# Linear attention with two gated MLPs on one core: prepared inputs through a DRAM scratch, their low halves on VectorE, output decays by a scan, two queues of work pinned

## The chip, the cores and the metric

The kernel runs on one core of a Trainium2 chip. The metric is device time in microseconds (us) of one execution, the median of several runs. The engines are named as in the profile: PE (TensorE, matrix products), PEld (its weight loads), DVE (VectorE), ACT (ScalarE), POOL (GpSimd), SP (SyncE, which here issues every DMA).

## What is computed

Inputs are six tensors of shape (4 batches, 8 heads, 768 steps, 40) and the weights of two MLPs. The first part is a recurrence over the 768 steps, for each of the 32 (batch, head) pairs, on a 40x40 state; its output, as 3072 tokens of 320 features, goes through two MLPs (320 to 2048 to 320), the second one with the gate h - tanh(h).

```python
for t in range(S):                                   # _attn_ref
    y[:, :, t] = np.einsum('bhd,bhde->bhe', rt, state)
    Sa = np.einsum('bhde,bhe->bhd', state, at)
    state_decay = state * wt[:, :, None, :] - np.einsum('bhd,bhe->bhde', Sa, bt)
    state = state_decay + np.einsum('bhd,bhe->bhde', vt, kt)
...
h = x @ w_in; g = h * (1.0 / (1.0 + np.exp(-h))); x = g @ w_out     # _moe_ref
h = x @ w_in; g = h - np.tanh(h);                 return g @ w_out  # _moe2_ref
```

## The kernel before

**Tiling.** The 768 steps are cut into 12 chunks of 64. Inside a chunk the recurrence becomes matrix products and one triangular inverse for each of the 32 pairs. A chunk is handled in two halves (hf) of 16 pairs; PE works on quarters (b = 0 to 3) of 8 pairs. Numbers that need more than half precision are kept as two f16 values, a high half (the rounded value) and a low half (what the rounding left), so that one f16 product over 120 rows holds three terms.

**The two stages.** Stage 1 runs the 12 chunks of the recurrence and, behind each chunk, the first MLP on its 256 tokens. Stage 2 (from `load_x2` on) is the second MLP for all 12 groups. The weights of both MLPs arrive as 64-bit floats and are taken apart and rebuilt by `conv_f32`, 32 conversions for each MLP, in stage 1; those of the second MLP are stored to a DRAM tensor `w2d` and read back at the start of stage 2.

**One chunk**, in the order of its data:
- `load_raw` (L195): SP loads a, (k, b), (r, v) and w of a half as 120 x 6 x 64 (120 = 3 groups of 40 features).
- `prep` (L210) for a half: DVE scans w into the running decay (L224) and its inverse (L230), multiplies a and (k, b) with them (L229, L233); POOL scales r and v (L193); ACT writes the high halves in f16 into the tile `HL`; POOL subtracts the low halves (`psub`, L190, and L239). Twelve SP transfers of 40 partitions each (L250) lay three planes (high, high or low, low) under each other in the tile `LR`, of which there are five buffers, two for a chunk. Four more transfers (L258) store the decay to the DRAM tensor `pd`. There is one buffer of `HL`.
- `p1` (L270): PE products of `LR`, taken out by DVE as `mK` (L278) and by ACT as `bP`. There is one PSUM buffer between PE and these.
- `sol_in`, 31 times `sol_step`, `sol_out` (L303 to L328): the triangular inverse on DVE. A transposition of `bP` into `Al` (L305) begins it; each step is a product (L314) and a sum (L316), 62 instructions in one chain; a transposition into `W1` (L326) ends it. `Al` and `Tl` have one buffer, so the inverse of the next chunk waits for this one's end.
- `mrg1`, `mrg2` (L334, L348), then the chain over chunks: `ch_x` (L364), `ch_u`, `ch_s`, `ch_y` (L423 to L432), `ch_m`. The buffer of `LR` is free when `ch_y` of its chunk and half has read it.
- `pf_load` (L483) reads the decay back from `pd` in three transfers in another layout, and `x_t2` (L506) multiplies the transposed output with it. Then `mm_h` (L569) and `mm_o` (L591) are the first MLP.

**Order.** Every step has a due time from the table `SC`, in units of an eighth of a chunk; steps are written in that order, and a scheduler then places each instruction on its engine's queue. Each queue runs in its order. `tc.issue_after(x)` holds what is written inside it behind instruction x on x's engine, without a wait for x's end. In the kernel before only the conversions of the first MLP are held that way (`conv_w1`, behind the first chunk's work). Those of the second (`conv_w2`, L553) have due times alone, and run between 197 and 605 us.

## Time and profile before

| | us |
|---|---|
| median of 3 runs (1231.36 to 1233.86) | 1231.57 |
| the profiled execution, its own time | 1226.61 |
| its span, from the first to the last instruction | 1224.9 |
| of the span: to the first inverse (L305 of chunk 0) | 38.6 |
| the inverses of chunks 0 to 11 (first L305 to last L326) | 747.3 |
| from there to the first product of stage 2 | 89.4 |
| stage 2 | 349.6 |

A row of the profile that groups instructions reads: line, engine, operation, output<-inputs, shapes, count | busy us, mean ns of one | idle time of the engine just before them and what ended it. Engines overlap, so that busy times do not add up to the span. A wait says which instruction an engine stood before, and whose end let it go.

### The profile page before, as it was taken

The page shows a single profiled execution, that of the slowest core. Times are in us where ns is not written, and L with a number is a line of the kernel's source. Part 1 is how long each engine was busy: PE and PEld are TensorE (multiplying, and loading weights), DVE is VectorE, ACT ScalarE, POOL GpSimd, SP SyncE. Part 2 cuts the span into 40 slices and gives each one's busy share as a digit, 9 for nine tenths or more (in the row PEclk, how much of TensorE's full clock was granted, in tenths as well). Part 3 has the DMA queues.
Part 4 walks back from the last instruction along what each step waited for, and adds up shares of the span by engine and source line. Part 5 has one row for each costly group of instructions (what it writes and reads, how often), then busy time and mean ns, then how long its engine had stood idle before and what let it go on. Part 6 is the DMA issues. An engine that isn't in the chain of part 4 may idle for free.

```text
span 1224.9 us, 32035 instructions
## 1 busy us (share of the span) xinstructions
PE 1035.7 (85%) x12624; PEld 861.4 (70%) x12624; DVE 943.0 (77%) x1847; ACT 819.7 (67%) x1586; POOL 402.9 (33%) x488
## 2 busy tenths in 40 slices
PE   0006659888989998988999999999899999999997
...
GB/s 161 180 195 180 176 157 148 142 160 139 162 114 153 138 140 159 128 176 127 123 105 118 106 80 73 31 37 25 224 27 25 25 36 25 25 25 31 18 12 23
DMA packets 187912, 126.35 MB, mean 103 GB/s; under 512 B 107696, under 2 KB 170224, under 8 KB 187760
## 3 DMA queue, kind: packets, MB, share of 16 engines
...
## 4 chain that ended last, share of the span: by engine, by line
PE 27%; issue 18%; DMA 16%; DVE 13%; POOL 11%; ACT 8%; SPq 7%; POOLq 0%; DVEq 0%; ACTq 0%
PE hp L569 8%; POOL gl L190 6%; SPq L250 4%; DMA LR<-HL 3%; DMA w2d<-w2s 3%; PE o L593 3%; PE o L591 3%; PE o L592 3%; DVE Tl L316 2%; DVE tmp L314 2%; ACT cr L527 2%; PE psx L364 2%; POOL HL L190 2%; DMA rawrv<-pk 2%; PE mg L348 1%
## 5 line engine op out<-in xcount | busy, mean ns | idle before, releaser
L569 PE MATMUL hp<-xh,wih 128*128 128x256 f16 x960 | 189.6, 283 | 6.1 <-DVE gl L579 4.4
L569 PE MATMUL hp<-x,w 128*128 128x256 f16 x1344 | 189.3, 273 | 3.1 <-DMA x<-x2d 3.1
L190 POOL TENSOR_TENSOR gl<-q,gh 128x512 f16<-128x512 f32 x96 | 111.8, 1165 | 221.6 <-ACT gh L626 219.7
L569 PEld LDWEIGHTS <-w 128*128 128x128 f16 x1344 | 131.4, 98 | 26.0 <-DMA x<-x2d 3.6
L569 PEld LDWEIGHTS <-wih 128*128 128x128 f16 x1344 | 129.1, 101 | 27.7 <-issue 4.5
L316 DVE TENSOR_TENSOR Tl<-Tl,tmp 128x126 f32<-128x126 f32 (+22 forms) x372 | 122.4, 329 | 7.8
L314 DVE TENSOR_TENSOR tmp<-Al,Tl 128x126 f32<-128x126 f32 (+22 forms) x372 | 118.2, 318 | 10.3 <-ACT Al L306 3.1
L270 PE MATMUL p1a<-LR 120*128 120x64 f16 x384 | 28.7, 206 | 107.8 <-DMA LR<-HL 67.3
L591 PE MATMUL o<-woh,gh 128*128 128x320 f16 x384 | 116.4, 304 | 0.8 <-DVE x2o L602 0.4
L592 PE MATMUL o<-woh,gh 128*128 128x320 f16 x384 | 116.3, 303 | 0.0
L593 PE MATMUL o<-woh,gl 128*128 128x320 f16 x384 | 115.1, 303 | 0.5 <-DVE gl L579 0.5
L591 PE MATMUL o<-w,gh 128*128 128x320 f16 x384 | 112.3, 301 | 1.3 <-ACT gh L626 1.3
L592 PE MATMUL o<-w,gh 128*128 128x320 f16 x384 | 113.4, 301 | 0.0
L569 PE MATMUL hp<-xl,wih 128*128 128x256 f16 x384 | 108.8, 283 | 0.0
L593 PE MATMUL o<-w,gl 128*128 128x320 f16 x384 | 103.3, 301 | 0.5 <-POOL gl L190 0.5
L270 PEld LDWEIGHTS <-LR 120*128 120x128 f16 x384 | 21.2, 104 | 115.1 <-issue 67.2
L621 DVE SCALAR_TENSOR_TENSOR s<-s,z 128x512 f32<-128x512 f32 x96 | 71.4, 744 | 33.9 <-ACT s L619 32.9
L593 PEld LDWEIGHTS <-gl 128*128 128x128 f16 x768 | 75.8, 99 | 28.0 <-issue 1.7
L591 PEld LDWEIGHTS <-gh 128*128 128x128 f16 x768 | 75.8, 99 | 27.5 <-ACT gh L626 1.6
L592 PEld LDWEIGHTS <-gh 128*128 128x128 f16 x768 | 75.8, 99 | 26.0 <-issue 0.8
L579 DVE SCALAR_TENSOR_TENSOR gl<-hp,gh 128x512 f16<-128x512 f32 x96 | 65.5, 683 | 34.5 <-ACT gh L578 34.0
L625 DVE COPY_PREDICATED q<-mk,t 128x512 f32<-128x512 int32 x96 | 79.1, 824 | 9.4
...
## 6 DMA issues: line engine op xcount, KB each, us to landing
...
```

The source lines that it names most:

```text
L190: POOL.tensor_tensor(out, a, b, ALU.subtract)
L250: SP.dma_start(out=dst[pl * 40:pl * 40 + 40, :, d0:d0 + w], in_=src[:, :, s0:s0 + w])
L270: PE.matmul(pa[:, p, :], kb, R[:, u, p, 0:C], start=True, stop=True)
L314: DVE.tensor_tensor(tv_, Al[:, j + 1:, j:j + 1].to_broadcast([128, n, w]), Tl[:, j:j + 1, :w].to_broadcast([128, n, w]), ALU.mult)
L316: DVE.tensor_tensor(Tl[:, j + 1:, :w], Tl[:, j + 1:, :w], tv_, ALU.add)
L569: PE.matmul(o, wi[:, f, a], x[:, k], start=n == 0, stop=False)
L579: DVE.scalar_tensor_tensor(out=gl, in0=hp, scalar=S_G, in1=gh, op0=ALU.mult, op1=ALU.subtract)
L591: PE.matmul(o, gh[:, cs], wo[:, f, 0], start=f == 0, stop=False)
L592: PE.matmul(o, gh[:, cs], wo[:, f, 1], start=False, stop=False)
L593: PE.matmul(o, gl[:, cs], wo[:, f, 0], start=False, stop=f == NF - 1)
L621: DVE.scalar_tensor_tensor(out=s, in0=s, scalar=GAMMA, in1=z, op0=ALU.add, op1=ALU.mult)
L625: DVE.copy_predicated(q, mk.bitcast(I32), t)
```

## The change

1. **Planes by way of DRAM.** `HL` holds its two parts (high and low) in rows that lie together. Two transfers of 120 partitions write them to a new DRAM tensor `pld`; three read them back into `LR`: two of 40 partitions and one of 80 partitions for the other planes. A half has five transfers in place of twelve, and the order of features inside the packed input changes to fit.
2. **Low halves by VectorE.** All four subtractions are DVE instructions. POOL's scaling of r and v is gone: ACT scales while it rounds, and DVE scales and subtracts in one instruction. POOL keeps no instruction of this step but the small `p63`.
3. **Output decays by a scan.** `pd`, its four stores and its three reads for a half are gone. The host adds an input `wf` (w in the layout of the outputs); `pf_load` is one load of it, and a new step `pf_scan` runs a DVE scan of 128 x 384 over it. The constant factor of `x_t2` moves into the scan's start value.
4. **Queues pinned.** `prep` of chunk c is held on DVE behind the last `ch_se` of chunk c - 3. `conv_w2` is held, on DVE, ACT, POOL and SP, behind marks of chunk 7 (conversions 0 to 9), 8 (10 to 19), 9 (20 to 29) and 10 (the rest): the last step of its inverse (DVE), the copy of `Al` (ACT), the clearing of `Tl` (POOL), the last transfer of its `prep` (SP). Its due times move accordingly.
5. The second scan of `prep` writes into the first one's tile (`pr` is gone).

```diff
@@ build @@
+    HL = at_p.tile([120, 2, 6, RW], F16, name="HL")
+    pld = dram.tile([nch, 2, 2, 40, 18, RW], F16, name="pld")
...
-        pscale(rrv, rrv, S_R)
-        ACT.activation(out=rh[:, :, C:2 * C], in_=rv, func=AF.Copy)
-        ACT.activation(out=lh[:, :, v0:v0 + C], in_=vv, func=AF.Copy)
-        (DVE if c == 0 else POOL).tensor_tensor(ll[:, :, k0:k0 + 2 * C], kb, lh[:, :, k0:k0 + 2 * C], ALU.subtract)
-        psub(rl[:, :, 0:C], av, rh[:, :, 0:C])
-        psub(ll[:, :, v0:v0 + C], vv, lh[:, :, v0:v0 + C])
-        psub(rl[:, :, C:2 * C], rv, rh[:, :, C:2 * C])
+        ACT.activation(out=rh[:, :, C:2 * C], in_=rv, func=AF.Copy, scale=S_R)
+        ACT.activation(out=lh[:, :, v0:v0 + C], in_=vv, func=AF.Copy, scale=S_V)
+        DVE.tensor_tensor(ll[:, :, k0:k0 + 2 * C], kb, lh[:, :, k0:k0 + 2 * C], ALU.subtract)
+        DVE.tensor_tensor(rl[:, :, 0:C], av, rh[:, :, 0:C], ALU.subtract)
+        for lo, x, hi, sc in ((ll[:, :, v0:v0 + C], vv, lh[:, :, v0:v0 + C], S_V), (rl[:, :, C:2 * C], rv, rh[:, :, C:2 * C], S_R)):
+            DVE.scalar_tensor_tensor(out=lo, in0=x, scalar=sc, in1=hi, op0=ALU.mult, op1=ALU.subtract)
...
-        for i in range(3):
-            n = 6 if i < 2 else 4
-            src, dst = hl[i * 40:i * 40 + 40, 0:n], LR[:, 6 * i:6 * i + n]
-            for pl, s0, d0, w in ((0, RW, 0, LW), (0, LW, LW, 2 * C), (1, RW, 0, RW), (2, 0, 0, RW)):
-                SP.dma_start(out=dst[pl * 40:pl * 40 + 40, :, d0:d0 + w], in_=src[:, :, s0:s0 + w])
+        for q in range(2):
+            SP.dma_start(out=pld[c, hf, q].rearrange("d (i j) n -> (d i) (j n)", i=3), in_=hl[:, q].rearrange("p j n -> p (j n)"))
+        for q, d0, w in ((0, 0, LW), (1, LW, 2 * C)):
+            SP.dma_start(out=LR[0:40, :, d0:d0 + w], in_=pld[c, hf, q, :, 0:16, d0:d0 + w])
+        SP.dma_start(out=LR[40:120].rearrange("p j n -> p (j n)"),
+                     in_=pld[c, hf].rearrange("q d j n -> (q d) (j n)")[:, 0:16 * RW])
...
+    def prep(c, hf):
+            for q in ((c - SC["pg"][2], "se") if c <= SC["pg"][3] else 0, ("sol", c - 1)):
+                if q in late:
+                    st.enter_context(tc.issue_after(late[q]))
...
+    def pf_scan(c, hf):
+        t = pf_t[c, hf].rearrange("p k n -> p (k n)")
+        DVE.tensor_tensor_scan(t, t, d1f.rearrange("p b t -> p (b t)"), 0.0, ALU.mult, ALU.add)
...
+    def conv_w2(pool, f, part):
+            c = SC["gate"][0] + int((2 * f + part) * SC["gate"][1])
+            for e in ("dve", "act", "pool", "sp"):
+                st.enter_context(tc.issue_after(late[min(c, nch - 1), e]))
```

**VectorE, from the end of the first chunk's preparation to the start of the first inverse.** Before (L278 is `mK` of chunk 0, L224 the first scan of chunk 1, L305 the transposition that begins the inverse):

```order
L233 TENSOR_TENSOR LR<-LR,pr 120x768
L239 TENSOR_TENSOR LR<-LR 120x6x128
L278 TENSOR_TENSOR mK_118<-p1a,mask_k 64x512 x4
L224 SCALAR_TENSOR_TENSOR pq<-raww,d1a 120x390
L305 STREAM_TRANSPOSE Al<-bP 64x1024
```

Now, the last rows of that stretch (L254 and L252 are low halves, L288 is `mK`, L246 the product of (k, b), L545 and L547 a conversion, L237 a first scan, here of chunk 2, L315 the transposition):

```order
L254 SCALAR_TENSOR_TENSOR HL<-rawrv,HL 120x6x64
L252 TENSOR_TENSOR HL<-rawa,HL 120x6x64
L254 SCALAR_TENSOR_TENSOR HL<-rawrv,HL 120x6x64
L288 TENSOR_TENSOR mK_121<-p1a,mask_k 64x512
L545 TENSOR_SCALAR cr<-cr 128x384
L547 SCALAR_TENSOR_TENSOR c_263<-c_263,cr 128x384
L288 TENSOR_TENSOR mK_121<-p1a,mask_k 64x512
L246 TENSOR_TENSOR rawkb<-rawkb,pq 120x768
L545 TENSOR_SCALAR cr<-cr 128x384
L237 SCALAR_TENSOR_TENSOR pq<-raww,d1a 120x390
L315 STREAM_TRANSPOSE Al<-bP 64x1024
```

Nearly the whole preparation of both halves of chunk 1 has moved ahead of the first inverse.

**SP, where a buffer of `LR` becomes free in the middle of stage 1.** Before (L393 are copies of `ch_u`, L559 and L517 belong to conversions, L450 and L451 carry the state to the next chunk):

```order
L250 DMA LR<-HL 40x6x194
L207 DMA VU_124<-tv 64x640
L250 DMA LR<-HL 40x6x128
L250 DMA LR<-HL 40x6x322 x2
L450 DMA MT<-MT 40x640
L451 DMA MT<-lows 40x640
L250 DMA LR<-HL 40x6x194
L250 DMA LR<-HL 40x6x128
L250 DMA LR<-HL 40x6x322 x2
L250 DMA LR<-HL 40x4x194
L250 DMA LR<-HL 40x4x128
```

Now (L468 and L469 carry the state; the stores of this half to `pld`, L260, stand about ten rows ahead):

```order
L409 DMA LR<-lows 40x16x64
L262 DMA LR<-pld 40x16x194
L262 DMA LR<-pld 40x16x128
L213 DMA VU_127<-tv 64x640
L263 DMA LR<-pld 80x5152
L468 DMA MT<-MT 40x640
L469 DMA MT<-lows 40x640
```

Three transfers wait for the buffer in place of twelve.

**VectorE, the end of the inverse of chunk 8.** Before (L314 and L316 are the step, L410 is `ch_se`, L326 begins its end):

```order
L410 TENSOR_TENSOR Sm<-pss,mask_s 128x512
L316 TENSOR_TENSOR Tl<-Tl,tmp 128x2x15
L440 SCALAR_TENSOR_TENSOR Md<-psm,p_6307 40x320
L314 TENSOR_TENSOR tmp<-Al,Tl 128x16
L316 TENSOR_TENSOR Tl<-Tl,tmp 128x16
```

Now (L326 and L328 are the step, L243 to L254 belong to `prep` of chunk 10, L545 to a conversion for the second MLP, L342 begins the end):

```order
L328 TENSOR_TENSOR Tl<-Tl,tmp 128x2x15
L243 SCALAR_TENSOR_TENSOR pq<-raww,d1b 120x389
L252 TENSOR_TENSOR HL<-rawa,HL 120x6x64
L326 TENSOR_TENSOR tmp<-Al,Tl 128x16
L246 TENSOR_TENSOR rawkb<-rawkb,pq 120x768
L288 TENSOR_TENSOR mK_122<-p1a,mask_k 64x512
L525 TENSOR_TENSOR pf<-psyt,pf 128x384
L328 TENSOR_TENSOR Tl<-Tl,tmp 128x16
L545 TENSOR_SCALAR cr<-cr 128x384
```

Preparation of a later chunk and conversions stand between and behind the last steps of the inverse, where before there were steps alone but for two instructions.

## Rows read from the trace of the kernel before

**Rows 1.** Windows: us, busy PE, PEld, DVE, ACT, POOL (count), clock, DMA share, GB/s.

```profile
0.00:38.60 38.60, 2.84 (x32) 2.04 (x32) 21.03 (x30) 9.51 (x17) 18.03 (x39) 1.00 0.59 156
38.60:169.00 130.40, 44.90 (x582) 40.97 (x582) 111.29 (x244) 84.94 (x164) 60.60 (x78) 0.82 0.66 178
169.00:508.20 339.20, 304.13 (x4276) 252.98 (x4274) 282.78 (x619) 236.51 (x475) 125.00 (x161) 0.93 0.55 147
508.20:752.30 244.10, 221.71 (x3281) 188.35 (x3281) 199.39 (x443) 148.79 (x302) 76.98 (x97) 0.97 0.44 117
752.30:785.90 33.60, 33.60 (x488) 28.38 (x488) 27.94 (x81) 19.23 (x39) 1.50 (x3) 1.00 0.15 36
785.90:875.30 89.40, 86.30 (x1158) 73.00 (x1157) 27.86 (x42) 37.71 (x77) 7.69 (x11) 1.00 0.30 89
```

**Rows 2.** Waits of DVE from 38 to 786 us: total us, times, longest.

```profile
DVE c L528 <- ACT cr L527: 13.7, 26, 2.2
DVE cr L526 <- ACT c L525: 12.8, 16, 1.9
DVE HL L226 <- DMA LR<-HL: 11.1, 9, 3.8
DVE mK L278 <- PE p1a L270: 10.9, 11, 2.3
```

**Rows 3.** Timeline and chain, from a freed buffer to the inverse of chunk 4.

```profile
282.05 0.19 PE L425 MATMUL psy<-M,LR 120*64 120x40 f16 x1
...
291.53 5.74 SPq L250 DMA_DIRECT2D LR<-HL  x7
...
296.50 2.55 DMA LR<-HL
...
310.26 1.95 DVE L305 STREAM_TRANSPOSE Al<-bP 64x1024 f32<-64x1024 f32 x1 [1.16 <-ACT bP L283]
```

**Rows 4.** DVE operations: ns of one, shortest/median/longest; then a group (busy us, mean).

```profile
L239 DVE TENSOR_TENSOR LR<-LR x1: 958/958/958, 22.7 to 22.7; 120x768 f16<-120x768 f32 x1
L229 DVE SCALAR_TENSOR_TENSOR rawa<-rawa,pq x23: 508/857/1696, 9.5 to 690.7; 120x384 f32<-120x384 f32 x23
L230 DVE TENSOR_TENSOR_SCAN pr<-raww,d1b x23: 949/955/1631, 10.0 to 692.2; 120x389 f32<-120x389 f32 x23
...
L229 DVE SCALAR_TENSOR_TENSOR rawa<-rawa,pq 120x384 f32<-120x384 f32 x23 | 20.3, 885 | 1.4 <-DMA rawa<-pk 1.4
```

**Rows 5.** POOL groups of the preparation: busy us, mean ns.

```profile
L190 POOL TENSOR_TENSOR HL<-rawrv,HL 120x384 f16<-120x384 f32 x46 | 48.3, 1061 | 2.5 <-ACT HL L237 2.4
L239 POOL TENSOR_TENSOR HL<-rawkb,HL 120x768 f16<-120x768 f32 x22 | 38.3, 1742 | 27.0 <-ACT HL L234 10.1 <-DMA pd<-pq 8.5 <-DMA LR<-HL 3.3
L190 POOL TENSOR_TENSOR HL<-rawa,HL 120x384 f16<-120x384 f32 x23 | 22.3, 969 | 31.1 <-ACT HL L235 30.8
L193 POOL TENSOR_SCALAR rawrv<-rawrv 120x768 f32<-120x768 f32 x23 | 22.1, 959 | 63.3 <-DMA rawrv<-pk 56.5 <-DMA x2d<-x2o 3.4 <-DMA rawa<-pk 3.2
```

**Rows 6.** Windows, busy DVE for the inverse's steps alone: chunk 11, sum of all.

```profile
755.60:784.50 28.90, 16.14 (x62) 1.00 0.17 42
sum 535.00, DVE 237.84; mean DVE 19.82
```

**Rows 7.** Timeline of DVE at the start: the last `mK` of chunk 0.

```profile
36.88 0.69 DVE L278 TENSOR_TENSOR mK<-p1a,mask_k 64x512 f32<-64x512 f32 x1 [2.15 <-PE p1a L270]
```

**Rows 8.** Timeline: end of the inverse and the merge, chunks 1 and 11.

```profile
164.53 1.95 DVE L326 STREAM_TRANSPOSE W<-Al 32x1024 f32<-32x1024 f32 x1 [0.57 <-ACT Al L323]
...
166.54 0.36 PE L334 MATMUL mg<-W,bP 32*32 32x32 f32 x3 [11.12 <-DVE W L326]
...
785.93 1.97 DVE L326 STREAM_TRANSPOSE W<-Al 32x1024 f32<-32x1024 f32 x1 [1.41 <-ACT Al L323]
...
803.32 0.47 PE L334 MATMUL mg<-W,bP 32*32 32x32 f32 x9
```

**Rows 9.** A store to DRAM in the chain: start us, us.

```profile
276.22 3.87 DMA w2d<-w2s
```

More of the change, by code (lines that the diff above doesn't have):

```diff
@@ L102, with build @@
     c1=(-9.2025, 0.5509, 0.821),
-    c2=(-43.8161, 0.9808),
+    c2=(8.0, 0.1),
+    gate=(7, 0.1),
+    pg=(3, -1, 3, 12),
 )
-def build(tc, pk, tv, w1i, w1o, w2i, w2o, out, nch=NCH, dbg=None):
+def build(tc, pk, tv, wf, w1i, w1o, w2i, w2o, out, nch=NCH, dbg=None):
     nc = tc.nc
@@ L148, in build @@
         msk[nm] = m
+    d1f = const.tile([128, 6, C], F16, name="d1f")
+    POOL.memset(d1f, 0.0)
+    POOL.memset(d1f[:, :, 0:1], P_INIT * S_X / (S_R * S_M))
     gam = const.tile([128, 1], F32, name="gam")
@@ L210, in prep, with prep_ @@
     def prep(c, hf):
+        with ExitStack() as st:
+            for q in ((c - SC["pg"][2], "se") if c <= SC["pg"][3] else 0, ("sol", c - 1)):
+                if q in late:
+                    st.enter_context(tc.issue_after(late[q]))
+            prep_(c, hf)
+    def prep_(c, hf):
         w, ra, rkb, rrv = raw_t.pop((c, hf))
@@ L229, in prep @@
         DVE.scalar_tensor_tensor(out=av, in0=av, scalar=-S_A * S_KB, in1=pq[:, :, 0:C], op0=ALU.mult, op1=ALU.mult)
-        DVE.tensor_tensor_scan(pr[:, 2:391][:, ::-1], w[:, 2:391][:, ::-1], d1b[:, 2:391][:, ::-1], 0.0, ALU.mult, ALU.add)
-        pi = pr[:, 2:392].rearrange("p (j t) -> p j t", t=65)[:, :, 0:C]
+        DVE.tensor_tensor_scan(pt[:, 2:391][:, ::-1], w[:, 2:391][:, ::-1], d1b[:, 2:391][:, ::-1], 0.0, ALU.mult, ALU.add)
+        pi = pt[:, 2:392].rearrange("p (j t) -> p j t", t=65)[:, :, 0:C]
         kbv = kb.rearrange("p j (q t) -> p j q t", q=2)
@@ L254, in prep @@
             gates["sp"] = nc.cur_bb.bb.instructions[-1]
-        for i, j0, n, u in ((0, 0, 6, 0), (1, 0, 2, 0), (1, 2, 4, 1), (2, 0, 4, 1)):
-            h = 6 * i + j0 - 8 * u
-            SP.dma_start(out=pd[c, hf, 40 * h:40 * (h + n), u].rearrange("(h d) t -> d h t", d=40),
-                         in_=pq[40 * i:40 * i + 40, j0:j0 + n, 0:C])
+        late[c, "sp"] = nc.cur_bb.bb.instructions[-1]
         p63 = at_p.tile([40, 2, 8, 1], F32, tag="p63", name="p63", bufs=5)
@@ L306, in sol_in @@
         ACT.activation(out=Al[64:128], in_=Al[0:64], func=AF.Copy)
+        late[c, "act"] = nc.cur_bb.bb.instructions[-1]
         POOL.memset(Tl, 0.0)
+        late[c, "pool"] = nc.cur_bb.bb.instructions[-1]
         for q in range(2):
@@ L318, in sol_step @@
             gates["dve"] = nc.cur_bb.bb.instructions[-1]
+        if j == SC["pg"][1] and c == 0:
+            late["sol", c] = nc.cur_bb.bb.instructions[-1]
+        if j == 30:
+            late[c, "dve"] = nc.cur_bb.bb.instructions[-1]
     def sol_out(c):
@@ L410, in ch_se @@
         DVE.tensor_tensor(sm, ps, msk["s"].unsqueeze(1).to_broadcast([128, 8, C]), ALU.mult)
+        if b == SC["pg"][0]:
+            late[c, "se"] = nc.cur_bb.bb.instructions[-1]
         ACT.activation(out=VU_t[c, hf][bb:bb + 64, u].rearrange("p (h d) -> p h d", d=D), in_=p2[bb:bb + 64],
@@ L484, in pf_load @@
         t = at_p.tile([128, 3, 128], F32, tag="pf", name="pf", bufs=1)
-        v = pd[c, hf].rearrange("f u t -> f (u t)")
-        SP.dma_start(out=t[:, 0:2], in_=v[0:256].rearrange("(k p) n -> p k n", k=2))
-        for q in range(2):
-            SP.dma_start(out=t[64 * q:64 * q + 64, 2], in_=v[256:320])
+        SP.dma_start(out=t, in_=wf[c, hf])
         pf_t[c, hf] = t
+    def pf_scan(c, hf):
+        t = pf_t[c, hf].rearrange("p k n -> p (k n)")
+        DVE.tensor_tensor_scan(t, t, d1f.rearrange("p b t -> p (b t)"), 0.0, ALU.mult, ALU.add)
     def x_t1(c, hf):
@@ L505, in x_t2 @@
         xf = pf_t.pop((c, hf))
-        DVE.scalar_tensor_tensor(out=xf, in0=ps, scalar=S_X * S_KB / (S_R * S_M), in1=xf, op0=ALU.mult, op1=ALU.mult)
+        DVE.tensor_tensor(xf, ps, xf, ALU.mult)
         ACT.activation(out=xh[:, :, cs], in_=xf, func=AF.Copy)
@@ L553, in conv_w2, with conv_w2_ @@
     def conv_w2(pool, f, part):
+        with ExitStack() as st:
+            c = SC["gate"][0] + int((2 * f + part) * SC["gate"][1])
+            for e in ("dve", "act", "pool", "sp"):
+                st.enter_context(tc.issue_after(late[min(c, nch - 1), e]))
+            conv_w2_(pool, f, part)
+    def conv_w2_(pool, f, part):
         t = pool.tile([128, 640], F16, tag="w2s", name="w2s", bufs=1)
```

25 lines of the change are left out of this document (14 added, 11 removed).

## The prediction

> **What bounds the kernel now.** I read the windows by stage first [rows 1], then the waits of the engine that is busy [rows 2], then one turn of the loop over chunks [rows 3]. Stage 2 (349.6 us) holds nothing that the change touches; everything is decided in the 875 us ahead of it. There the windows show two engines near their limit at once. From the first inverse to the start of the last transposition out of it (38.6 to 785.9 us) DVE is busy for 111.3 + 282.8 + 199.4 + 27.9 = 621.4 of 747.3 us, 83%. The last inverse, where POOL is idle and little else is queued, shows the same 83% (27.9 of 33.6): the remainder there is hand-overs to ACT and gaps between dependent steps. So 83% is about DVE's full rate, in every one of the four windows. PE is at 304 of 339 us and 222 of 244 us in the middle two, and at 100% from 752 us on. POOL is busy for a quarter to a half of the time, and yet matters: the 62 steps of an inverse cost 16.1 us in chunk 11 beside an idle POOL, and 237.8 / 12 = 19.8 us on the mean [rows 6]; the same multiplication of 384 elements takes 0.51 us at its shortest and 0.86 at its median [rows 4].
>
> The loop: a buffer of LR falls free at 282.2 us (the last product of ch_y of chunk 2); the transfers into it are issued until 297.3 and the last lands at 299.1; the next inverse begins at 310.3 [rows 3]. Two chunks further the same buffer order comes round, 133 us later on this stretch by the period of the windows (339.2 / 5 = 67.8 a chunk).
>
> **The change part by part.** The profiled execution took 1226.6 us, 5.0 less than the median; the sum is made against it and carried to the median.
>
> *Low halves and scan on DVE: dearer.* 22 subtractions of 768 at 0.96 us (two of the 24 are on DVE already), 72 of 384 at 0.51 and 24 scans at 0.955 [rows 4]: 21.1 + 36.7 + 22.9 = 80.7 us. At the median of the loaded instructions (0.86) it would be 106; it cannot be below 80.
>
> *POOL emptied: cheaper for DVE.* 48.3 + 38.3 + 22.3 + 22.1 = 131 us of POOL go [rows 5], of 282 us that it is busy up to 785.9 [rows 1], 46%. How long DVE is held up by POOL: in the steps 237.8 - 12 x 16.1 = 44 us [rows 6], in L229 20.3 - 23 x 0.508 = 8.6 [rows 4], 53 in all, in groups with 258 of DVE's 621 us. If the other 363 us are exposed half as much, that is 53 + 37 = 90; not at all, 53; as much, 128. I take 90, since the longest of L230 is 1.63 against 0.95. Of that 46% go: -41 (bounds -24 and -59). Net on DVE +40, bounds +22 to +82.
>
> *Where it lands.* By the order, chunk 1's preparation, the first low halves, a scan and a conversion, 17 us at these durations, now stand ahead of the first inverse, where DVE is busy for only 21 of 38.6 us. The cost there is the delay of the first inverse: half 1 of chunk 0 needs 5.5 us more of DVE work (some of it in idle time), then a store to DRAM at 3.9 [rows 9] and a load at 2.6 [rows 3] in place of a transfer that began as soon as its plane was ready; the last mK stood at 36.9 [rows 7]. Together +5, bounds 0 and +10. The remaining 40 - 17 = 23 us stand in the 747 us, at 83%: +28.
>
> *Five transfers for twelve, and none for the decays.* SP issues in a row: the seven L250 in 5.74 us are 0.82 each [rows 3]. Behind the freed buffer there are three issues in place of twelve, so about 7.4 us less; the load of two planes in one transfer is larger, and I allow it 2 us more than the 2.55 of the last small one. So the buffer is full some 5 to 8 us sooner, each two chunks. The path to the inverse gets this only where it waits for it: DVE waits 10.9 us for the products p1 (L278), and 11.1 for HL, which a transfer to LR held and which a store to DRAM now frees without any LR buffer [rows 2]. I take all of the second and half of the first: -17, bounds 0 (PE's order has other work in front) and -45 (a rival, below). ACT's and SP's other work is unchanged or less and hidden behind DVE; the larger f32 reads of ACT's scaling cost nothing that a row shows.
>
> A page speaks against this part. The Trainium skill, "DMA: Bandwidth & Descriptors", section "Latency and other measured facts", says that most of a transfer's fixed 2 us is the receipt from the target memory, and that HBM is the slowest target, up to 2 us under load. The trace agrees in sign: the store to DRAM took 3.9 us, the transfer inside the chip 2.6 [rows 9, 3]. By the page one would count an estimated 2 us or more for each of 24 halves, 48, if all were on the path; the sum above does not, since from chunk 1 on the stores stand well ahead of their loads in SP's order.
>
> *Conversions of the second MLP held back.* Some 25 of 32 move from the middle to the inverses of chunks 8 to 10. Their DVE work is the same. Their waits (13.7 + 12.8 us for all 64 conversions [rows 2]) go with them. I count 0, with the gain in the middle and the loss later as the two rivals.
>
> *The end.* In chunk 1 PE starts the merge 2.0 us after the inverse's last transposition begins; in chunk 11 it comes 17.4 us after, since PE is behind with the first MLP [rows 8]. DVE may be up to 15 us later there at no cost. And by the order 24 products of mm_o (some 0.14 us each at their spacing, an estimate) have moved ahead of that point: -3. So -18, if DVE does come later; bounds -3 and -18.
>
> Sum: +5 + 28 - 17 - 18 = **-2 us**: 1224.6 profiled, about **1230** as a median. In words: the work that DVE takes over is paid for by POOL's silence, the idle start and PE's backlog at the end.
>
> **The rivals.**
> - *Faster: the buffer loop sets the period.* If LR, not DVE's rate, holds the period, each two chunks get 8 us shorter from chunk 3 on, 4 x 9 = 36, and the middle also loses the conversions' waits. PE's idle time is the floor: 35 us from 169 to 508 and 22 after [rows 1], so at most 57 and hardly over 40. With the start's +5 that is -31: **1200**. For it: the inverse begins 11 us after the last landing [rows 3], and the chain of waits holds transfers for a good part. Against it: DVE's 83% everywhere.
> - *Slower: the conversions crowd the late inverses.* By the order, chunks 8 to 10 hold about 30 conversions and the preparation of 10 and 11 stands between the last steps of the inverse, where a step waits for the step before. At 1 us of DVE and 0.4 of waiting each, 25 more conversions are +35 there; six halves of preparation and eight scans add 6 x 2.5 + 8 x 0.95 = 23; at 83%, +66 on the 244 us. The middle gives back at most 339 - 304 - 15 = 20, as PE holds it, the end 18, the start costs 5: +33, and +25 if some hides in DVE's waits: **1256**. It decides from the point where those four chunks take more than 280 us in place of 244.
> - *Slower still: POOL was not the cause of the long DVE durations.* Then DVE carries +81, not +40: 41 / 0.83 = +49: **1279**. For it: no row shows the two engines side by side. Against it: the steps beside an idle POOL are the shortest [rows 6].
>
> **How the numbers follow.** About 0.2% (2.5 us) is what a measurement of this kernel tells from no change; the runs before spread that far. Forecast (own range 1217 to 1243, from the bounds of the start, the net of DVE and the end) 0.46; loop 0.28; crowding 0.21; POOL not the cause 0.05. The forecast's own range straddles the line: faster 0.18, same 0.16, slower 0.12. Faster is then 0.18 + 0.28 = 0.46, same 0.16, slower 0.12 + 0.26 = 0.38. The range reaches over most of both first rivals: 1200 to 1256, with a tenth left out on either side.
>
> **What would show it.** Right: DVE's busy time up to the last inverse higher by 25 to 50 us with the steps of an inverse near 17.5 us; POOL near 150 us there; the first inverse at 40 to 48 us; the wait of L226 (now L239) for a transfer gone; the merge of chunk 11 within 8 us of its transposition; SP with three issues behind each freed buffer. The loop rival: a period under 62 us from chunk 3 to 7 that is kept afterwards. The crowding rival: four chunks 7 to 11 at over 280 us with DVE above 85%, and ACT waiting for conversions. The forecast is wrong at its root if DVE's busy share falls well below 83% while the time falls too, since then waits, not work, set the pace.

## The result: 1.2% slower

The changed kernel takes 1247.05 us (median of four runs, 1244.63 to 1249.33); the kernel before, beside it, 1231.81. The ratio is 1.012, with a 95% interval of 1.0096 to 1.0144. The prediction was 1230, with "faster" and "no change" together at 0.62: the direction was missed, the time lies in the range. The profiled execution has a span of 1244.1 us, 19.2 more than that of before. (The profiled execution of before was 5 us faster than its median, so that 19 us in the profiles stand for 15 in the medians.)

Windows of the profile after, cut at the same events as [rows 1] (columns as there: PE, PEld, DVE, ACT, POOL, clock, DMA share, GB/s):

```profile
0.00:55.40 55.40, 2.33 (x32) 1.95 (x32) 34.88 (x61) 17.03 (x31) 10.87 (x36) 1.00 0.90 227
55.40:178.10 122.70, 40.28 (x581) 37.51 (x582) 100.19 (x241) 73.77 (x144) 34.36 (x47) 0.83 0.73 185
178.10:500.10 322.00, 295.26 (x4227) 249.46 (x4226) 268.15 (x618) 195.87 (x392) 51.94 (x77) 0.93 0.55 138
500.10:773.70 273.60, 243.09 (x3381) 203.71 (x3380) 231.79 (x532) 195.47 (x396) 72.97 (x99) 0.90 0.64 169
773.70:807.10 33.40, 33.40 (x521) 29.19 (x518) 28.43 (x84) 19.59 (x37) 1.52 (x3) 1.00 0.14 36
807.10:893.30 86.20, 80.92 (x1079) 68.25 (x1078) 28.87 (x43) 36.66 (x76) 7.71 (x11) 0.99 0.32 94
```

The first inverse begins 16.8 us later (55.4 against 38.6), chunk 2's 9.1 later (178.1), chunk 7's 8.1 earlier (500.1 against 508.2), chunk 11's 21.4 later (773.7 against 752.3). So three things happened one after the other: a loss of 16.8 us at the start, a gain (7.7 us in chunks 0 and 1, 17.2 in chunks 2 to 7), and a loss of 29.5 in chunks 7 to 11, where the second MLP's conversions now stand. In that last stretch PE's granted clock was also lower (0.90 against 0.97), and PE was busy for 243.1 us with 3381 products where it had been busy for 221.7 with 3281; how much of the 29.5 us is due to the clock is not shown. DVE's busy time in the inverses' stretch is 628.6 us against 621.4, POOL's 160.8 against 264.1.

Waits of DVE after, from 55 to 807 us (us in total, times, longest), to be set against [rows 2]:

```profile
DVE pf L508 <- DMA pf<-wf: 13.2, 9, 2.9
DVE cr L545 <- ACT c L544: 10.1, 14, 1.7
DVE mK L288 <- PE p1a L280: 10.1, 9, 2.5
DVE c L547 <- ACT cr L546: 9.1, 17, 1.0
...
DVE HL L254 <- DMA pld<-HL: 3.7, 3, 1.8
DVE HL L239 <- DMA pld<-HL: 3.2, 7, 0.7
```

The wait for HL fell from 11.1 to 6.9 us (3.2 + 3.7); the forecast had counted on all of it. A wait for the load of the decays into `pf` stands in its place; nothing in the forecast had one there.

The steps of the inverses after, all twelve, as in [rows 6]:

```profile
sum 593.50, DVE 207.26; mean DVE 17.27
```

They take 207.3 us for all 744 instructions. The windows of [rows 6] held 734 of the 744; all of them took 240.6 before. The multiplication of 384 elements [rows 4] has its median at 0.544 us in place of 0.857, and its mean at 0.612 in place of 0.885:

```profile
L242 DVE SCALAR_TENSOR_TENSOR rawa<-rawa,pq x23: 510/544/1133, 10.4 to 690.3; 120x384 f32<-120x384 f32 x23
L242 DVE SCALAR_TENSOR_TENSOR rawa<-rawa,pq 120x384 f32<-120x384 f32 x23 | 14.1, 612 | 0.0
```

The last merge, as in [rows 8] (timeline, start and duration):

```profile
807.14 1.99 DVE L342 STREAM_TRANSPOSE W<-Al 32x1024 f32<-32x1024 f32 x1 [0.17 <-ACT Al L339]
...
822.24 1.19 PE L350 MATMUL mg<-W,bP 32*32 32x32 f32 x32
```

PE comes to it 15.1 us after the transposition. It was 17.4 before, and the forecast wanted "within 8".

### The profile page after: what moved, and what is told of

The parts are those of the page before. It is cut to its first block, busy times and chain, and to the rows that moved or that the text cites. A ratio compares the mean times of both kernels' runs of the same rounds, so it can differ in the third digit from the quotient of the medians.

```text
span 1244.1 us, 31466 instructions
## 1 busy us (share of the span) xinstructions
PE 1038.6 (83%) x12624; PEld 866.3 (70%) x12624; DVE 966.9 (78%) x1965; ACT 821.2 (66%) x1586; POOL 291.7 (23%) x372
## 3 DMA queue, kind: packets, MB, share of 16 engines
q1 hardware_dynamic: 140192, 142.60, 44.5%
## 4 chain that ended last, share of the span: by engine, by line
PE 28%; issue 17%; DMA 12%; POOL 9%; DVE 6%; ACT 5%; SPq 2%; POOLq 0%; DVEq 0%; ACTq 0%
PE hp L595 8%; POOL gl L196 7%; DMA LR<-pld 4%; PE o L619 3%; PE o L618 3%; PE o L617 3%; DMA pf<-wf 2%; PE psx L380 2%; PE psu L395 2%; DMA pld<-HL 2%; DMA w2d<-w2s 2%; PE psy L441 2%; PE mg L364 1%; POOL w2s L196 1%; PE hp L596 1%
## 5 line engine op out<-in xcount | busy, mean ns | idle before, releaser
L326 DVE TENSOR_TENSOR tmp<-Al,Tl 128x126 f32<-128x126 f32 (+22 forms) x372 | 106.1, 285 | 8.8 <-ACT Al L316 1.2
L280 PE MATMUL p1a<-LR 120*128 120x64 f16 x384 | 24.3, 209 | 102.7 <-DMA LR<-pld 77.1
L328 DVE TENSOR_TENSOR Tl<-Tl,tmp 128x126 f32<-128x126 f32 (+22 forms) x372 | 101.2, 272 | 8.2
L647 DVE SCALAR_TENSOR_TENSOR s<-s,z 128x512 f32<-128x512 f32 x96 | 72.0, 750 | 38.6 <-ACT s L645 37.6
L617 PEld LDWEIGHTS <-gh 128*128 128x128 f16 x768 | 75.8, 99 | 29.5 <-ACT gh L652 2.0
L196 POOL TENSOR_TENSOR lows<-Md,MT 40x320 f16<-40x320 f32 x44 | 43.3, 983 | 216.4 <-ACT MT L465 107.7
## 6 DMA issues: line engine op xcount, KB each, us to landing
pld<-HL SPq DMA_DIRECT2D x46, 452.8 KB
LR<-pld SPq DMA_DIRECT2D x24, 805.0 KB
LR<-pld SPq DMA_DIRECT2D x24, 242.5 KB
```

What stands on the lines that cost most here:

```text
L196: POOL.tensor_tensor(out, a, b, ALU.subtract)
L280: PE.matmul(pa[:, p, :], kb, R[:, u, p, 0:C], start=True, stop=True)
L326: DVE.tensor_tensor(tv_, Al[:, j + 1:, j:j + 1].to_broadcast([128, n, w]), Tl[:, j:j + 1, :w].to_broadcast([128, n, w]), ALU.mult)
L328: DVE.tensor_tensor(Tl[:, j + 1:, :w], Tl[:, j + 1:, :w], tv_, ALU.add)
L617: PE.matmul(o, gh[:, cs], wo[:, f, 0], start=f == 0, stop=False)
L647: DVE.scalar_tensor_tensor(out=s, in0=s, scalar=GAMMA, in1=z, op0=ALU.add, op1=ALU.mult)
```

## Experiments

The kernel before ran beside each of them on the same chip, and the ratios are to it. Single executions differ (the ten of e1 lie between 1227.1 and 1237.7 us), so verdicts go by the ratios, and a profile only tells where. "2 to 7" and "7 to 11" are the us between the starts of those chunks' inverses.

| kernel | ratio, 95% interval | first inverse | 2 to 7 | 7 to 11 |
|---|---|---|---|---|
| before | 1 | 38.6 | 339.2 | 244.1 |
| after | 1.012, 1.0096 to 1.0144 | 55.4 | 322.0 | 273.7 |
| e1: after, chunk 0 direct | 0.9977, 0.9955 to 1.0000 | 39.3 | 315.7 | 275.3 |
| e2: after, conversions spread | 1.0195, 1.0164 to 1.0227 | 54.8 | 340.0 | 268.4 |
| e3: after, no scratch | 1.0046, 1.0025 to 1.0066 | 40.0 | 310.4 | 274.8 |
| e4: after, no hold of prep | 1.0355, 1.0324 to 1.0386 | 54.7 | 336.5 | 254.8 |
| f1: after, prep of chunk 1 held | 1.0077, 1.0046 to 1.0107 | 52.5 | 311.3 | 275.6 |
| f2: before, low halves on DVE | 1.0129, 1.0091 to 1.0168 | 39.9 | 354.8 | 241.0 |
| f3: before, conversions held | 1.0086, 1.0050 to 1.0121 | 39.4 | 320.6 | 265.9 |
| f4: e1, low halves on POOL | 0.9982, 0.9951 to 1.0014 | 39.7 | 321.2 | 272.5 |
| g1: before, delay in chunk 0 | 1.0187, 1.0141 to 1.0234 | - | - | - |
| g2: before, delay in chunk 5 | 1.0170, 1.0123 to 1.0217 | - | - | - |
| g3: before, delay in chunk 11 | 1.0026, 0.9998 to 1.0054 | - | - | - |
| g4: e1, decays' scan due later | 0.9986, 0.9959 to 1.0013 | 39.6 | 317.9 | 275.6 |
| h1: e1, conversions a chunk later | 0.9960, 0.9941 to 0.9979 | 38.8 | 314.7 | 265.2 |
| h2: e1, conversions from chunk 5 | 1.0022, 1.0000 to 1.0044 | 40.3 | 327.4 | 268.0 |
| h3: after, half 1 of chunk 0 direct | 0.9988, 0.9959 to 1.0016 | 49.2 | 325.8 | 270.8 |
| i1: h1, decays' scan held | 0.9979, 0.9959 to 0.9999 | 39.0 | 311.0 | 267.1 |
| i2: h1, low halves on POOL | 0.9942, 0.9908 to 0.9975 | 40.3 | 320.5 | 262.7 |

### The start

**e1.** Chunk 0 alone goes from HL to LR directly:

```diff
+        if c == 0:
+            for i in range(3):
+                n = 6 if i < 2 else 4
+                src, dst = hl[i:120:3], LR[:, 6 * i:6 * i + n]
+                for pl, q, d0, w in ((0, 0, 0, LW), (0, 1, LW, 2 * C), (1, 0, 0, RW), (2, 1, 0, RW)):
+                    SP.dma_start(out=dst[pl * 40:pl * 40 + 40, :, d0:d0 + w], in_=src[:, q, 0:n, d0:d0 + w])
+        else:
...
```

> The changed kernel with the transfers of chunk 0 alone as before (twelve from the tile HL to the tile LR for each half, no DRAM scratch there); all else is the changed kernel, whose profiled first inverse began at 55.4 us (before: 38.6) and whose median is 1247. Theory S (start): PE's idle time up to stage 2 grew by 16 us, nearly all of it ahead of the first inverse, so the delayed start passes through to the end: first inverse at 39 to 43, time 1231 to 1235. Theory L (late crowding): by chunk 7 the changed kernel had already made up the start and was 8 us ahead, and chunks 7 to 11 then took 273.6 us in place of 244.1, so the late conversions and the late preparation set the end: first inverse early too, but the inverse of chunk 11 within 5 us of the 773.7 it has now, time 1241 to 1247.

The ratio fell from 1.012 to 0.998: with chunk 0's transfers direct the whole loss is gone. Chunks 7 to 11 are as long as ever (275.3), so theory L is out as the cause of it. This does not say that the rest of the change costs nothing: put alone into the kernel before, two of its parts cost 1.3% and 0.9% (f2 and f3 below); either other parts make up for them in the whole change, or the parts do not add up. The start of the changed kernel, in the timelines of SP and of PE:

```profile
29.08 0.32 SPq L260 DMA_DIRECT2D pld<-LR  x1
...
36.46 0.70 SPq L262 DMA_DIRECT2D LR<-pld  x1
37.22 1.51 SPq L263 DMA_DIRECT2D LR<-pld  x1
...
47.86 0.58 PE L280 MATMUL p1a<-LR 120*128 120x64 f16 x8 [12.00 <-DMA LR<-pld]
```

Half 1 was prepared at 29 us. The last store was issued at 29.08 and landed 7.1 us later, and the first load that waited for it was issued at 36.46; the last load, issued at 37.2, landed at 47.8, 10.5 us later. My bounds had taken 3.9 and 2.6 for them, from a store of 160 KB and a load inside the chip. In the windows, the DMA share of that stretch:

```profile
27.70:55.40 27.70, 2.33 (x32) 1.95 (x32) 15.76 (x28) 10.53 (x20) 2.56 (x5) 1.00 0.97 254
```

The DMA engines are full there (0.97, against 0.59 up to the first inverse before), and they have more to carry. From the page after, the issues and their sizes:

```profile
pld<-HL SPq DMA_DIRECT2D x46, 452.8 KB
LR<-pld SPq DMA_DIRECT2D x24, 805.0 KB
```

A half moves 2 x 452.8 + 805.0 + 242.5 + 160 = 2113 KB, where the three planes alone are 1208 (120 rows of 16 x 322 values of two bytes). The large load is long not only at the start. Later in the chain it took 6.65 to 9.94 us, and the DMA engines were 0.88 to 1.01 busy while it ran; in the chain and the windows of the shortest and the last:

```profile
498.60 6.65 DMA LR<-pld
...
751.77 8.60 DMA LR<-pld
...
498.60:505.20 6.60, 2.61 (x46) 1.76 (x45) 6.26 (x9) 5.37 (x11) 0.67 (x1) 0.80 0.89 210
751.80:760.40 8.60, 4.95 (x66) 4.09 (x64) 8.05 (x16) 6.73 (x12) 2.66 (x6) 1.00 0.88 180
```

**f1** splits this: `late["sol", 0]` is set to the last `mK` of chunk 0, which holds chunk 1's preparation, and so its work on DVE and its stores, behind it.

```diff
+        if c == 0 and b == 3:
+            late["sol", 0] = nc.cur_bb.bb.instructions[-1]
```

> The changed kernel (DRAM scratch for chunk 0 too) with the preparation of chunk 1 held on VectorE behind the last mK of chunk 0, so that its instructions and its stores to the scratch come behind chunk 0's, as in the kernel before. It splits the 16.8 us by which the first inverse came later. If the stretch is lost to traffic (the DMA engines were busy for 0.96 to 0.97 of 27.7 to 55.4 us, with two stores of 453 KB of chunk 1 among it): first inverse at 43 to 47, 1234 to 1240. If it is lost on the path itself (a store that waits for the whole half, 7.1 us for it, 10.5 us for the load of 805 KB): first inverse at 49 to 54, 1241 to 1247.

It is the path: first inverse at 52.5, ratio 1.008. Chunk 1's transfers and DVE work together account for 3 of the 16.8 us; with them gone, half 1 still has its last store landed 7.8 us after its issue and its last load 8.5 us after its own, and its products start at 44.5 us in place of 47.9. In the timeline of PE of f1:

```profile
33.26 0.59 PE L280 MATMUL p1a<-LR 120*128 120x64 f16 x8 [33.26 <-DMA LR<-pld]
...
44.54 0.59 PE L280 MATMUL p1a<-LR 120*128 120x64 f16 x8 [8.32 <-DMA LR<-pld]
```

**h3** sends half 1 directly, half 0 through the scratch (the condition of e1 becomes `c == 0 and hf == 1`).

> The changed kernel with half 1 of chunk 0 alone sent directly; half 0 goes through the scratch. In the changed kernel the first products of half 0 came at 32.9 us (before: about 24) and those of half 1 at 47.9 (33). If half 1's own way is what counts: first inverse at 39 to 44, ratio 0.998 to 1.002. If half 0's stores and loads also hold up half 1's transfers in the queue of SP: first inverse at 45 to 50, ratio 1.003 to 1.008.

The two markers disagree: the first inverse came at 49.2, out of the 39 to 44 of the first reading, and yet the ratio is that of e1. The lateness is not half 1's own way. Its first products start at 38.32, but its second ones only at 44.10, behind `bP`, which ACT takes out of PSUM after two conversions of the first MLP that had waited for their weights. In the timelines of PE and ACT of h3:

```profile
38.32 0.58 PE L287 MATMUL p1a<-LR 120*128 120x64 f16 x8 [2.53 <-DMA pld<-HL]
...
42.51 0.54 ACT L551 ACTIVATE c<-cr 128x384 f32<-128x384 f32 x1 [0.50 <-DMA cr<-w1i]
43.08 0.59 ACT L299 ACTIVATE bP<-p1a 32x512 f32<-32x512 f32 x1
...
44.10 0.59 PE L287 MATMUL p1a<-LR 120*128 120x64 f16 x8 [5.19 <-ACT bP L300]
```

Why this lateness costs nothing is not shown. The start of chunk 1's inverse fits (101.3 us, against 100.3 before, 106.2 after and 101.7 in e1), but it does not order all runs: in f1 it is 115.5, and f1 is no slower than after.

### The price of a delay

**g1, g2, g3** put the same six transpositions more into the kernel before, in chunk 0, 5 or 11 (in g1 the condition reads `c == 0`, and so on):

```diff
-        DVE.transpose(out=Al[0:64], in_=bP[bb:bb + 64, :, 0:32].rearrange("p h t -> p t h"))
+        for _ in range(7 if c == 0 else 1):
+            DVE.transpose(out=Al[0:64], in_=bP[bb:bb + 64, :, 0:32].rearrange("p h t -> p t h"))
```

> The kernel before with the transposition that begins the inverse of chunk 0 made seven times in place of once (6 x 1.9 = 11.5 us more of VectorE, the same values). The forecast let PE's backlog at the last merge take up to 15 us of any delay of VectorE: within 3 us of the kernel before. If a delay ahead of the first inverse passes through, because PE stands idle meanwhile and lacks that time later: +9 to +13, as the changed kernel's start did (16.8 us later, 15 us slower).

> The same six transpositions more, in chunk 5, the middle. The forecast's end term: within 3 us of the kernel before. If the middle is bound by VectorE's rate and the end takes nothing: +9 to +13. If PE's queue holds enough work there to go on: +3 to +7, with PE's idle time after the first inverse (146 us now) up by as much.

> The same six transpositions more, in chunk 11, the last. PE is at 100% there and begins the merge 17.4 us after the inverse's last transposition, so both readings expect nothing: within 3 us of the kernel before, and the merge 4 to 8 us after that transposition. If the lag is not a slack (PE had reached the merge and stood before it for another reason): +9 to +13.

The expectations counted 11.5 us for the six. Other work was placed between them, so that the last one stood 18.8, 18.0 and 14.0 us behind the first; in the timeline of DVE of g1, the first and the last of the seven:

```profile
39.40 1.90 DVE L306 STREAM_TRANSPOSE Al<-bP 64x1024 f32<-64x1024 f32 x1
...
58.23 1.95 DVE L306 STREAM_TRANSPOSE Al<-bP 64x1024 f32<-64x1024 f32 x1
```

The times rose by 1.87%, 1.70% and 0.26%: 23, 21 and 3 us (95% intervals 17 to 29, 15 to 27 and 0 to 7). So a delay of the inverse in the first or the middle chunk passes through in full, and in the last chunk it is nearly free. The reason stands in the last transposition and the last merge, in the timelines of g1 and then of g3:

```profile
809.79 1.95 DVE L327 STREAM_TRANSPOSE W<-Al 32x1024 f32<-32x1024 f32 x1 [1.49 <-ACT Al L324]
...
827.12 1.19 PE L335 MATMUL mg<-W,bP 32*32 32x32 f32 x32
```

```profile
811.98 1.99 DVE L327 STREAM_TRANSPOSE W<-Al 32x1024 f32<-32x1024 f32 x1
...
815.28 1.20 PE L335 MATMUL mg<-W,bP 32*32 32x32 f32 x32
```

With the delay in chunk 0, PE still comes 17.3 us after the transposition; with the delay in chunk 11, 3.3. The lag was 15.3 in g2 and 15.1 in the changed kernel. The reading that fits: PE's backlog is work that earlier chunks hand it; when they are late the backlog is late too, and takes up nothing. A part of a delay that arises near the end is taken up: in e1 the last transposition came 16.1 us later than before and the lag was 9.8.

PE's own time says the same. The windows up to stage 2 of before, after and e1:

```profile
0.00:875.30 875.30, 693.48 (x9810) 585.72 (x9811) 670.29 (x1455) 536.69 (x1071) 289.81 (x389) 0.94 0.50 134
0.00:893.30 893.30, 695.28 (x9811) 590.06 (x9812) 692.31 (x1574) 538.40 (x1072) 179.36 (x273) 0.92 0.59 152
0.00:884.50 884.50, 702.59 (x9810) 596.14 (x9811) 695.97 (x1573) 539.31 (x1071) 171.09 (x273) 0.92 0.58 151
```

PE has the same products to make in each, and is idle for 181.8, 198.0 and 181.9 us. Up to the first inverse it was idle for 35.8 us before and 53.1 after, so the 16.2 us more are those of the start, and nothing behind it made them good. In e1 they are gone. What e1's profile is longer by is PE's busy time, at a lower granted clock (0.92 against 0.94).

### The conversions and the holds

**e2** (`gate=(2, 0.25)` in place of `(7, 0.1)`):

> The changed kernel with one number pair altered: the conversions for the second MLP are held behind chunk 2 + n/4 in place of chunk 7 + n/10, so that about four stand in each inverse from chunk 3 to 10, in place of 7 to 10 in each from chunk 8 to 10. Theory L (late crowding): chunks 7 to 11 fall from 273.6 to about 250 us, chunks 2 to 7 grow from 322 to at most 332: time 1232 to 1238. Theory S (start): the start is untouched and PE is the bound behind it: 1244 to 1249, what chunks 7 to 11 lose is found again in chunks 2 to 7.

Both theories miss: slower by 0.75% than after. The middle grew by 18 us, the late chunks fell by 5. In its windows (chunks 2 to 7, then 7 to 11) PE's granted clock, a mean over its two levels (1.2 and 2.4 GHz), is 0.88 of full speed in both, against 0.93 and 0.90 after, and PE is busy for 10 us more with the same number of products in the first:

```profile
177.80:517.70 339.90, 305.17 (x4224) 258.34 (x4223) 288.55 (x654) 231.16 (x459) 77.33 (x105) 0.88 0.59 155
517.70:786.10 268.40, 243.35 (x3377) 206.05 (x3375) 220.69 (x496) 163.13 (x328) 50.61 (x72) 0.88 0.55 141
```

**f3** puts the hold of the conversions alone into the kernel before (`c2`, `gate` and the four marks of the change).

```diff
-    c2=(-43.8161, 0.9808),
+    c2=(8.0, 0.1),
+    gate=(7, 0.1),
@@ conv_w2 @@
+            for e in ("dve", "act", "pool", "sp"):
+                st.enter_context(tc.issue_after(late[min(c, nch - 1), e]))
```

> The kernel before with part 4's hold of the second MLP's conversions alone (behind chunks 7 to 10, due times as in the changed kernel). Crowding theory: the inverses of chunks 8 to 11 grow by 20 to 35 us, the middle gives back 10 to 20: 1240 to 1255. If the hold pays (the changed kernel with the conversions spread from chunk 3 on was slower by 0.75%): 1218 to 1228. If it only moves time from one stretch to another: 1229 to 1235.

Its windows (chunks 2 to 7, 7 to 11, the last inverse):

```profile
172.20:492.90 320.70, 297.37 (x4278) 250.88 (x4277) 259.58 (x568) 193.40 (x386) 99.14 (x124) 0.94 0.43 113
492.90:758.80 265.90, 230.71 (x3336) 193.25 (x3333) 214.34 (x478) 179.24 (x358) 88.48 (x118) 0.96 0.52 140
758.80:805.10 46.30, 41.80 (x588) 35.27 (x589) 36.11 (x102) 36.70 (x76) 12.01 (x18) 0.96 0.43 126
```

The middle gave back 18.5 us, the late chunks took 21.8, the last inverse 12.7 (46.3 us in place of 33.6), and the time rose by 0.9%. The crowding theory had these sizes: 18.5 of the 34.5 us are only moved, and the rest is a cost (16 us in the profile, 11 by the ratio).

**h1** and **h2** move the conversions in the kernel with the repaired start: `gate=(8, 0.1)` and `gate=(5, 0.16)`.

> As e1_c0_direct (ratio 0.998), with the conversions for the second MLP held one chunk longer (behind chunk 8 + n/10), so that some 9 of 32 come into the last inverse and behind it, where six transpositions more cost only 0.3%. If the crowding is a net cost that the free end can take: ratio 0.988 to 0.994, chunks 7 to 11 at 255 to 265 us in place of 275. If time is only moved: 0.996 to 1.001. If the conversions in the last inverse cost more there, since the weights of stage 2 come later or the merge does: 1.002 or above.

> As e1_c0_direct, with the conversions spread over chunks 5 to 9 (held behind chunk 5 + 0.16 n; five to seven in each inverse). If late crowding is a net cost: 0.988 to 0.995. If time is only moved: 0.996 to 1.001, chunks 7 to 11 shorter than 275 us by as much as chunks 2 to 7 are longer than 316. If spreading costs, as it did from chunk 3 on with the scratch in chunk 0: 1.003 to 1.008.

With the conversions from chunk 5 on, the ratio is 1.0022, with 7 0.9977, with 8 0.9960. So 8 is better than 5, with some ten of 32 in the last inverse and behind it, where g3 found delays to be nearly free; 7 and 8 can't be told apart. h1 lies at the edge of "time is only moved", h2 between that and "spreading costs". In the kernel before, the late hold cost 0.9% (f3); why it does better than an earlier one here is not settled, and no run has the changed kernel with the conversions as they were before. The windows of h1, cut the same way:

```profile
172.20:486.90 314.70, 291.45 (x4222) 248.83 (x4220) 268.11 (x615) 193.42 (x386) 51.88 (x74) 0.92 0.56 140
486.90:752.10 265.20, 237.56 (x3422) 199.74 (x3421) 223.47 (x514) 179.01 (x362) 57.38 (x84) 0.95 0.62 158
752.10:796.00 43.90, 38.13 (x507) 31.95 (x505) 36.10 (x99) 32.07 (x68) 10.22 (x16) 0.81 0.45 131
```

The late stretch is 10 us shorter than in e1, the last inverse 7 us longer. In h2 the middle is 11.7 us longer than in e1 and the late stretch 7.3 shorter.

**e3** sends every chunk directly (e1's six lines, without the condition), **e4** drops the hold of `prep` (`pg=(3, -1, 3, -1)`):

> The changed kernel with the DRAM scratch gone for every chunk: twelve transfers from HL to LR for each half as before; low halves on VectorE, decays by the scan and both holds stay. If the scratch is what costs (it moves 2113 KB for a half in place of 1208), the start (39 to 43) comes back and the loads behind a freed buffer are no longer 7 to 10 us long: 1225 to 1233. If the scratch pays apart from the start, by three issues in place of twelve and by freeing HL early, the wait of about 11 us for HL and some 7 us for each second chunk return in the middle: 1240 to 1255.

> The changed kernel without the hold of the preparation on VectorE (the hold of the conversions stays). By the order the preparation then runs up to five chunks ahead and is over by chunk 4. If the late preparation is half of the crowding (23 us of DVE work in chunks 7 to 11 by the forecast's count), chunks 7 to 11 get some 20 us shorter and chunks 1 to 4 longer by as much or more: 1240 to 1255. If the hold is free: 1245 to 1249. If the hold delays transfers that the inverse waits for: 1235 to 1240.

e3 is 0.7% slower than e1: apart from chunk 0 the scratch pays some 8 us. Its profile does not show where, for its chunks 2 to 7 are shorter than those of e1. The expectation had both sides half right: the start came back (40.0), and the rest was not 1240 us or more. In e4 the preparation runs ahead of the chain, and chunk 2's inverse begins at 212.9 us. With the scratch the hold is needed: without it the kernel is 2.3% slower. That it is the scratch which makes it so, since HL no longer waits for a buffer of LR, is argued; no run drops both. Without the hold chunks 7 to 11 took 254.8 us, but chunks 0 to 7 lost more than twice what they gained (549.4 us to chunk 7 in place of 500.1).

### The low halves and the new wait

**f2** puts the four low halves of the change, with ACT's scaling, alone into the kernel before; **f4** is e1 with the old lines of that step (POOL's scaling and three `psub`).

```diff
-        pscale(rrv, rrv, S_R)
-        (DVE if c == 0 else POOL).tensor_tensor(ll[:, :, k0:k0 + 2 * C], kb, lh[:, :, k0:k0 + 2 * C], ALU.subtract)
-        psub(rl[:, :, 0:C], av, rh[:, :, 0:C])
...
+        DVE.tensor_tensor(ll[:, :, k0:k0 + 2 * C], kb, lh[:, :, k0:k0 + 2 * C], ALU.subtract)
+        DVE.tensor_tensor(rl[:, :, 0:C], av, rh[:, :, 0:C], ALU.subtract)
...
```

> The kernel before with part 2 of the change alone: all low halves on VectorE, scaling in ScalarE's rounding. The forecast's term: 58 us of DVE work more (22 x 0.96 + 72 x 0.51), less what POOL no longer holds up; at the forecast's 41 that is +17 net, at 83% +20, less some at the start and the end: 1238 to 1248. If POOL's silence is worth 60, as the changed kernel's DVE total says (24 us more in place of 81): within 3 of the kernel before. If POOL was not the cause: 1265 or more.

> The changed kernel with chunk 0's transfers direct (as e1_c0_direct, whose ratio was 0.998) and the low halves back on POOL with its scaling of r and v, as before. If VectorE's low halves cost on balance: ratio 0.985 to 0.993. If POOL's contention is worth just as much: 0.995 to 1.001. If POOL's silence is worth more than the 58 us of work: 1.005 or above, with longer steps of the inverse again (19 to 20 us a chunk in place of 17).

f4 equals e1 in time. Its steps do not: with POOL busy for 279.3 us in place of 155.0 in that stretch, and only the low halves and the scaling moved, they are a sixth longer, and DVE is busy for 6.3 us more with 88 instructions less. The steps of f4 and then of e1, from the first inverse to the last transposition:

```profile
39.70:789.20 749.50, 243.51 (x744) 0.91 0.62 158
39.30:802.10 762.80, 210.17 (x744) 0.90 0.61 155
```

In f2, from the first inverse to the last transposition:

```profile
39.90:808.20 768.30, 615.18 (x8647) 522.60 (x8648) 624.37 (x1472) 491.41 (x976) 150.23 (x229) 0.90 0.50 134
```

DVE has 88 instructions more there than before, and is busy for 624.4 us against 621.4; its steps take 213.2. The 88 took 57.0 us, so the silence of POOL is worth 54 of them, and of the 21 us by which the stretch is longer 18 are DVE's idle time. Why that grew here and not between e1 and f4 isn't settled: the order of the conversions moved forward too (between the first instructions of chunk 2's and chunk 3's inverse, eight of their stores in place of four).

**g4** and **i1** go for the wait for `pf`. g4 changes the due times of the scan to (6.0, 7.1); i1 has these due times too, and holds the scan, on top of h1:

```diff
+            st.enter_context(tc.issue_after(late[c, "se"]))
+            pf_scan_(c, hf)
```

> The changed kernel with chunk 0's transfers direct (as e1_c0_direct, ratio 0.998) and later due times for the scan of the outputs' decays (6.0 and 7.1 in place of 2.4 and 5.4), so that VectorE does not come to it before its load has landed: that wait was the longest of VectorE in the changed kernel, 13.2 us in all, where before it stood 11.1 us for HL. If that wait is on the path: ratio 0.986 to 0.992. If PE's work is the bound behind the start: 0.995 to 1.001.

> As h1_c0_direct_gate8 (ratio 0.996), with the scan of the outputs' decays held on VectorE behind the last ch_se of its chunk; the scans of half 0 then come some 100 instructions later, when their load has long landed. If the wait for that load (15 us in all with half 0 and half 1) is on the path: the wait falls to 8 us or less and the ratio to 0.988 to 0.992. If VectorE only waits there in place of waiting elsewhere: 0.994 to 0.999.

g4 decides nothing: the scan stayed where it was and the wait was 15.2 us again. In i1 it fell from 15.0 (h1) to 3.9, and the time did not fall. DVE waits elsewhere in its place.

```profile
DVE pf L520 <- DMA pf<-wf: 3.9, 4, 1.4
```

**i2** joins what had shown itself best: h1 with the low halves on POOL.

> As h1_c0_direct_gate8 (ratio 0.996), with the low halves back on POOL. By f4 against e1 (0.998 both) the two ways cost the same: 0.994 to 0.999. If VectorE's work counts in the late chunks, which are 84% busy: 0.988 to 0.993. If POOL, which then has conversions and low halves, holds up the late chunks: above 1.0.

0.9942, the lowest ratio here: i2 and h1 beat both kernels. Whether i2 beats h1 isn't told (0.9908 to 0.9975 against 0.9941 to 0.9979).

## Why the prediction was wrong, by its own steps

| term | forecast | measured, profile |
|---|---|---|
| start, to the first inverse | +5 | +16.8 |
| DVE's work in the inverses' stretch | +28 (23 / 0.83) | +7.2 |
| transfers and stalls: DVE's idle time there | -17 | -2.8 |
| end, to stage 2 | -18 | -3.2 |
| stage 2 | 0 | +1.2 |
| sum | -2 | +19.2 |

The second row's forecast is 23 us of work and 5 of idle time with it; the measured value is busy time alone. Together the second and third rows were forecast at +11 and came at +4.4. So the stretch of the inverses was better than forecast by 6.6 us, and the misses are the end (14.8) and the start (11.8).

**The end was the largest miss, and a step of reasoning, not a size.** I read PE's lag of 17.4 us at the last merge [rows 8] as a slack that any delay of DVE could use. g1 to g3 show it is one for delays of the last inverse only, and PE's idle time up to stage 2 that the start's loss came through in full. Without the term the forecast would have been +16, close to what came, but by luck: the start was 11.8 us too low and the stretch 6.6 too high. The forecast's own bound for the end, -3, would have given 1245, above the "own range" of 1217 to 1243. The rows alone could have raised the doubt: the lag was 2.0 us in chunk 1 and 17.4 in chunk 11, so it had built up on the way, and would again.

**The start** was rightly named and a third of its size. The bounds (0 and +10) rested on the nearest rows [rows 9, 3], whose transfers carried 160 KB and a twelfth of a half; those here carry 453 and 805, one behind the other, and a store waits for the whole half where each of the twelve began when its plane was ready. Bytes and the DMA share (0.59 already) could have set the upper end. The page of the Trainium skill that I weighed against this part ("DMA: Bandwidth & Descriptors", section "Latency and other measured facts") speaks of a store's receipt, up to 2 us; by it two halves would cost an estimated 4 us. The runs show larger times, 7.1 us for the store where the forecast took 3.9 and 10.5 for the load where it took 2.6; no run separates the receipt in them. Nor does one separate the bytes from the queue of other transfers: in f1, with chunk 1's gone and a DMA share of 0.88 from 27.7 to 40.0 us, they were 7.8 and 8.5.

**DVE's work:** 34.9 - 21.0 = 13.9 of it came ahead of the first inverse (17 forecast). In the stretch 7.2 us in place of 23 are left, and the sign "higher by 25 to 50" failed: of the 80.7 us taken over, 13.9 + 7.2 = 21.1 were added, so POOL's silence was worth 60 us where I took 41, just past the upper bound I gave (59). f2 has 54 for the low halves alone. The steps at 17.3 us are the forecast's 17.5. The rival "POOL was not the cause" is out by f4 and e1.

**Transfers and stalls:** of the 17 us, 11.1 were the wait for HL and the rest half of that for p1. The first fell by 4.2, the second by 0.8 (10.1 against 10.9), and the wait for the load into `pf` rose from 2.1 to 13.2. A freed buffer was full sooner, as forecast: ahead of the inverse of chunk 5 it fell free at 348.0, three issues followed at once, and the last landed at 359.9, 12 us in place of the 17 of [rows 3] (one turn of each kernel). But the issues were only part of the price. In the timelines of PE and SP and in the chain, the last load takes 9.9 us where the small one took 2.55:

```profile
347.82 0.19 PE L443 MATMUL psy<-M,LR 120*64 120x40 f16 x1
...
348.05 0.83 SPq L262 DMA_DIRECT2D LR<-pld  x2
350.00 0.58 SPq L263 DMA_DIRECT2D LR<-pld  x1
...
350.00 9.94 DMA LR<-pld
```

e1 against e3 credits the scratch, outside chunk 0, with 0.7%, 8 us of the 17.

**The rivals.** The loop rival wanted a period under 62 us from chunk 3 to 7; it is 63.8 there, and 68.4 from 7 to 11. The middle's gain does not need the buffer's: e3, with twelve transfers, has its chunks 2 to 7 at 310.4 us, and the kernel before with nothing but the conversions held (f3) at 320.6. The crowding rival had the right place and the right sign: 273.6 us in place of 244 (its threshold was 280), DVE at 85%, the middle shorter by 17 (at most 20 forecast). It counted +66 where +29.5 came (its own sum, 58 / 0.83, is 70), and in f3 about half of what the late chunks took came back from the middle. I gave it 0.21 and the loop 0.28; the middle's gain and the late loss came together and should have been priced together. In e1 both are still in place, and the time is that of before: what decided was the start.
